# Finer first projections, an early half-sum of two score tiles and narrower last columns in a fused attention and gated MLP kernel

## The chip, the cores and the metric

The kernel runs on one NeuronCore of a Trainium2 chip. The metric is the device time of one execution in microseconds (us); the time before is the median of 3 runs, 195.9 us (195.79 to 197.63). The engines are named as in the profile: PE is the TensorE matrix engine, PEld its weight loads, DVE is VectorE, ACT is ScalarE, POOL is GpSimd and SP is SyncE, which here only issues DMAs.

## The reference

One transformer block on a sequence of S = 2048 rows, D = 512, in bf16:

```python
h  = x + attn(layernorm(x)) @ wo           # 32 heads of 16, q,k,v = layernorm(x) @ wqkv
h2 = h + (relu(h_n @ W_gate) * (h_n @ W_up)) @ W_down      # h_n = layernorm(h), F = 1376
# attn: row s looks at the 8 rows s, s-2, ..., s-14 (rows below 0 are masked)
logits = einsum("bhsd,bhswd->bhsw", q, k_gathered) * 16**-0.5
o      = einsum("bhsw,bhswd->bhsd", softmax(logits), v_gathered)
```

## The kernel before

**Chunks.** The rows are worked on in four chunks (0 to 3) of 512 rows. Activations lie transposed, features on the 128 partitions and rows along the free axis, in tiles of [128, 4, 512] called quad. A chunk passes through these steps; the names are those of the plan in the code, with the chunk's number behind a point (sc1.3 is step sc1 of chunk 3).

- xst, xag, xxn, xtp: layernorm of x and its transposition on PE (chunk 3's goes through SP's DMA transpose).
- qkv0 to qkv11 (line 572): the twelve projections of 128 output features, each 4 matmuls of 512 columns over the depth of 512. Numbers 0 to 7 are q and k in turn for feature group t = 0 to 3; 8 to 11 are v. ACT evicts each from its PSUM bank (line 580). In chunk 0 the first NHALF of the q, k projections are split in three parts, a (rows 0 to 255, depth parts 0 and 1), b (the same rows, depth parts 2 and 3) and c (rows 256 to 511), of 256 columns each, so that they can run before all rows are there.
- pr0, pr1 (line 620, in chunk 0 line 637 in halves): DVE multiplies q by four shifted copies of k into a tile big of [128, 8, 512]: two feature groups t, t+1 in one tile, four window places each. pr0 is for the window places 0 to 3, pr1 for 4 to 7. There are two such tiles for each.
- sc0, sc1 (line 628): PE sums the features of each head with a 0/1 matrix sel of 32 columns: 8 matmuls for a tile big, 16 for both, each on a quarter of the PE array's columns, into one bank. ex0, ex1 on ACT take exp of it.
- es (DVE, line 728) adds the two exp tiles and den (PE) sums them over the window with one matmul; a chunk that is not in DEN1 has no es, and den takes two matmuls instead (line 716). dl and dr (ACT) make the reciprocal; am0, am1 (DVE, line 740) multiply the exp tiles by it in chunks 1 to 3.
- bd0, bd1 (SP, line 756): 4 DMAs each copy the weights out to all features. mu0 to mu3 (DVE, line 788, in chunk 0 line 803): weights by v, four tiles big. ta (POOL, line 831) or tree (DVE, line 791) adds the upper half of a big to its lower half, and tree goes on to 1: chunks 0 to 2 do the first step by an accumulating DMA of POOL, chunk 3 on DVE.
- wo (line 867), rs, layernorm hnm, hsq, hxn (lines 448, 456, 502), transposition htp on PE or htd on SP, in parts.
- mm0 to mm5 (lines 940 and 907): gate and up, 4 matmuls of 512 columns each; mm5 is the tail of 96 features (line 907). ue and ge (ACT) evict, gu (DVE, line 968) multiplies. dn (line 990): down projection, four row blocks a chunk, each 11 matmuls, in a first part of 8 and a second of 3. o (DVE line 1003 or ACT line 999) adds the residual or evicts, os stores (line 1009 or 1027).

**The order.** Each step is an Op with an engine. RANK holds one number for each Op in the order of its creation; on each engine the Ops run in the order of their numbers, and nothing else moves one ahead of another. Buffers are given out by a plan with durations written in the code: 5 tiles big, 9 quad, 8 PSUM banks, 5 row, 3 ex. An engine that reaches a step whose input or buffer is not ready waits, and everything behind it on that engine waits too.

**The end.** In chunk 3 the last row block of dn is made in pieces of columns, cut at LASTC: 0 to 255 and 256 to 511, each with its own add (line 1003) and its own store.

PRH names pairs of q*k tiles, (chunk, pr0 or pr1, first feature group), whose two feature groups are added before sc: sc then takes 4 matmuls for the tile rather than 8. Before, PRH is empty. With "V" the add is done by DVE (line 654), in place.

Of the kernel before, what the change touches and what calls it, by code (L numbers as in the profile page):

```python
# [17 lines left out]
RANK = [  # L18
# [38 lines left out]
]  # L57


# [33 lines left out]
class Plan:  # L93
# [9 lines left out]
    def add(self, key, *a, **k):  # L103
        op = Op(*a, **k)
        op.key = key
        op.seq = len(self.ops)
        if RANK:
            op.prio = RANK[op.seq]
        self.ops.append(op)
        for b in set(op.take) | set(op.use):  # L110
            b.left += 1
        return op
# [90 lines left out]
def kernel(  # L203
# [12 lines left out]
    Bsz, S, D = A_x.shape  # L216
# [5 lines left out]
    W = 8  # L222
    DIL = 2
    PADL = 16
    DEN1 = (1, 2, 3)
    BCD = {(0,0):"SSSS",(0,1):"SSSS",(1,0):"SSSS",(1,1):"SSSS",(2,0):"SSSS",(2,1):"SSSS",(3,0):"SSSS",(3,1):"SSSS"}
    PRE = ()
    PRD = ()
    PRH = {}
    ODA = (0, 1)  # L230
    LATE = "ud"
    NAB = 0
# [64 lines left out]
    V = nc.vector  # L297
# [75 lines left out]
    PRS, MUH = (0,), (0,)  # L373
    TDD, TDL = 1.3, 1.5
    NWARM, NFILL = 56, (13, 10, 0)
    NHALF = 6
    XT = (3.47, 3.64, 5.45, 5.97, 8.4, 8.7, 9.25, 9.75, 15.9, 17.65)
    WT = (7.65, 7.65, 5.0, 13.7, 19.0, 24.95, 22.4, 28.8)
    DMAT = (('h',2,0),('h',2,2),('h',3,0),('h',3,2),('h',1,0),('x',3,0),('x',3,2))
# [12 lines left out]
    HSP = ()  # L392
    TMT = (0, 1, 2, 3)
    TTM, DTG, ATE = 0.0845, 0.35, 0.3
    LASTC = (D // 2,)

    LNA = ((0, 1, 0, 1), (0, 0, 0, 0))

# [156 lines left out]
    for tk in range(NCK):  # L555
# [10 lines left out]
        for n, (c, t) in enumerate(seq):  # L566
# [15 lines left out]
            wl = wload["qkv"[c]][0]  # L582
            if tk == 0 and n < NHALF:

# [21 lines left out]
        for hf in range(2):  # L606
            sc, ex = Buf(at_s), Buf(ex_s)
            scd, prd = [], []
            for t in range(0, NT, 2):
# [12 lines left out]

                hs = PRH.get((tk, hf, t))

# [62 lines left out]
            elif tk in MERGE:  # L687
                scd = [add(("sc%d" % hf, tk), "PE", (4 - sum((tk, hf, t) in PRH for t in (0, 2))) * MM + SW, lambda p=prd: [f() for _, _, f in p],
                           [a for a, _, _ in prd], apr, take=[sc], use=[b for _, b, _ in prd], lat=PEL)]
# [21 lines left out]
        def f_dn(exs=exs, dn=dn, tk=tk, es=None):  # L711
            if tk in DEN1:
                nc.tensor.matmul(dn.t[:], lhsT=(same if tk in EARLY else spread)[:], rhs=es.t[:], start=True, stop=True)  # L713
                return
            for hf in range(2):
                nc.tensor.matmul(dn.t[:], lhsT=(same if tk in EARLY else spread)[:], rhs=exs[hf].t[:], start=(hf == 0), stop=(hf == 1))  # L716
# [6 lines left out]

        if tk in DEN1:
            es = Buf(es_s)
# [250 lines left out]
        if tk == NCK - 1:  # L976
            cs = (0,) + LASTC + (D,)
            parts[-1:] = [(BPC - 1, a, b) for a, b in zip(cs, cs[1:])]
# [98 lines left out]
```

## Time and profile before

| | |
|---|---|
| median of 3 runs | 195.9 us |
| profiled execution, whole | 196.0 us |
| its span, first to last instruction | 193.7 us |
| granted TensorE clock | 1.000 |
| PE busy | 188.5 us (97%) |
| DVE busy | 147.2 us (76%) |
| ACT busy | 115.2 us (59%) |

A row of the timeline gives start, duration, engine, line, operation, shapes and how many instructions are merged in it; a row of the chain that ended last gives start, duration, engine and line. "[0.56 <-ACT kT L580]" means that the engine was idle for 0.56 us and that the last thing to release it was ACT's write of kT on line 580. A matmul's own duration (379 ns for 512 columns) is longer than the step from one matmul to the next, since matmuls overlap; the chain gives the steps.

### The profile page before, as it was taken

The page shows a single profiled execution, that of the slowest core. Times are in us where ns is not written, and L with a number is a line of the kernel's source. Part 1 is how long each engine was busy: PE and PEld are TensorE (multiplying, and loading weights), DVE is VectorE, ACT ScalarE, POOL GpSimd, SP SyncE. Part 2 cuts the span into 40 slices and gives each one's busy share as a digit, 9 for nine tenths or more (in the row PEclk, how much of TensorE's full clock was granted, in tenths as well). Part 3 has the DMA queues.
Part 4 walks back from the last instruction along what each step waited for, and adds up shares of the span by engine and source line. Part 5 has one row for each costly group of instructions (what it writes and reads, how often), then busy time and mean ns, then how long its engine had stood idle before and what let it go on. Part 6 is the DMA issues. An engine that isn't in the chain of part 4 may idle for free.

```text
span 193.7 us, 3083 instructions
## 1 busy us (share of the span) xinstructions
PE 188.5 (97%) x1120; PEld 99.0 (51%) x1139; DVE 147.2 (76%) x239; ACT 115.2 (59%) x241; POOL 17.4 (9%) x35
## 2 busy tenths in 40 slices
PE   7999999999999999999999999999999999999993
PEld 7986455555436435454444554444445444545452
DVE  6889999999999999999997679999564401134331
ACT  3489898965999673965156649623478712435500
POOL 3000002330000013100044001003000000000000
PEclk9999999999999999999999999999999999999999
DMA  6799564999902609917579974135101624001102
GB/s 205 242 296 376 138 155 93 192 196 260 353 5 49 171 14 199 191 33 170 122 143 194 180 192 90 29 80 94 18 0 27 162 58 135 0 27 54 30 23 86
DMA packets 25070, 24.61 MB, mean 127 GB/s; under 512 B 11136, under 2 KB 21344, under 8 KB 25056
## 3 DMA queue, kind: packets, MB, share of 16 engines
q1 hardware_dynamic: 22032, 16.23, 30.1%
q0 software_dynamic: 2304, 7.34, 20.8%
q10 hardware_dynamic: 720, 0.85, 1.2%
q8 instruction: 9, 0.15, 0.3%
q14 instruction: 5, 0.04, 0.1%
HBM read 8.42 MB, written 2.10 MB: 54 GB/s over the span
## 4 chain that ended last, share of the span: by engine, by line
PE 97%; ACT 1%; issue 1%; DVE 0%; ACTq 0%
PE bank L940 35%; PE bank L572 21%; PE bank L990 20%; PE bank L867 7%; PE bank L628 4%; PE bank L421 3%; PE bank L907 3%; PE bank L531 2%; PE bank L429 1%; ACT up_sb L944 1%; PE bank L870 0%; PE bank L713 0%; PE bank L716 0%; DVE row L1003 0%; ACT vT L580 0%
## 5 line engine op out<-in xcount | busy, mean ns | idle before, releaser
L940 PE MATMUL bank<-quad,wgu_sb 128*128 128x512 bf16 x312 | 72.4, 379 | 0.4
L940 PEld LDWEIGHTS <-wgu_sb 128*128 128x128 bf16 x320 | 31.0, 98 | 36.4 <-issue 1.0
L990 PE MATMUL bank<-wd_sb,gT 128*128 128x512 bf16 (+2 forms) x185 | 39.6, 366 | 0.1
L944 ACT CAST up_sb<-bank 128x512 bf16<-128x512 f32 x40 | 22.3, 590 | 22.2 <-PE bank L940 20.5
L572 PE MATMUL bank<-quad,wqk_sb 128*128 128x512 bf16 (+1 forms) x148 | 29.4, 344 | 0.3
L947 ACT ACTIVATE gr<-bank 128x512 bf16<-128x512 f32 x40 | 23.5, 606 | 9.5 <-PE bank L940 5.2
L968 DVE TENSOR_TENSOR gT<-gr,up_sb 128x1024 bf16<-128x1024 bf16 x20 | 13.8, 688 | 19.4 <-ACT up_sb L944 10.5
L990 PEld LDWEIGHTS <-gT 128*128 128x128 bf16 (+1 forms) x187 | 18.2, 98 | 19.8 <-DVE gT L968 0.2
L620 DVE TENSOR_TENSOR big<-quad,kT 128x4096 bf16<-128x4096 bf16 x12 | 27.2, 2284 | 0.2 <-ACT kT L580 0.2
L788 DVE TENSOR_TENSOR big<-big,vT 128x4096 bf16<-128x4096 bf16 x12 | 27.1, 2285 | 0.2 <-PE bank L940 0.2
L572 PEld LDWEIGHTS <-wqk_sb 128*128 128x128 bf16 x152 | 16.7, 113 | 10.3 <-issue 0.2
L831 POOL DMA_DIRECT2D big<-big x12 | 10.5, 904 | 81.7 <-DVE big L788 54.2
L791 DVE TENSOR_TENSOR big<-big 128x1024 bf16<-128x1024 bf16 (+2 forms) x24 | 16.9, 728 | 0.0
L572 PE MATMUL bank<-quad,wv_sb 128*128 128x512 bf16 x61 | 15.3, 380 | 0.2
L867 PE MATMUL bank<-wo_sb,quad 128*128 128x512 bf16 x62 | 15.0, 379 | 0.1
L1003 DVE TENSOR_TENSOR row<-x_sm,bank 128x512 bf16<-128x512 bf16 (+1 forms) x9 | 5.5, 627 | 12.2 <-PE bank L990 12.2
L456 ACT ACTIVATE row<-x_sm,mv 128x512 bf16<-128x512 bf16 x12 | 8.6, 718 | 7.2 <-DVE mv L448 7.1
L547 ACT COPY quad<-bank 128x1024 bf16<-128x1024 bf16 (+1 forms) x10 | 8.6, 898 | 7.2 <-PE bank L531 7.2
L878 DVE SCALAR_TENSOR_TENSOR x_sm<-x_sm,bank 128x512 bf16<-128x512 bf16 x12 | 8.2, 687 | 4.9 <-PE bank L867 4.7
L580 ACT CAST kT<-bank 128x512 bf16<-128x512 f32 x16 | 9.1, 597 | 3.3 <-PE bank L572 1.8
L467 DVE BATCH_NORM_STATS2 st<-x_sm 128x6 f32<-128x512 bf16 x16 | 10.2, 675 | 0.4 <-DMA x_sm<-in_A_x_dram 0.4
L580 ACT CAST quad<-bank 128x512 bf16<-128x512 f32 x16 | 9.5, 602 | 1.6 <-PE bank L572 1.5
(77 smaller groups left out, 169.5 us busy)
## 6 DMA issues: line engine op xcount, KB each, us to landing
big<-big POOLq DMA_DIRECT2D x12, 512.0 KB, 5.3
big<-ex SPq DMA_DIRECT2D x32, 128.0 KB, 2.8
wgu_sb<-in_B_W_gate_dram SPq DMA_DIRECT2D x2, 688.0 KB, 7.7
wgu_sb<-in_B_W_up_dram SPq DMA_DIRECT2D x2, 688.0 KB, 7.5
wd_sb<-in_B_W_down_dram SPq DMA_DIRECT2D x2, 640.0 KB, 7.9
x_sm<-in_A_x_dram SPq DMA_DIRECT2D x2, 512.0 KB, 5.1
x_sm<-up_sb POOLq DMA_DIRECT2D x4, 256.0 KB, 3.8
out_dram<-x_sm SPq DMA_DIRECT2D x4, 256.0 KB, 2.3
```

Of the source, the lines that this page charges most:

```text
L572: nc.tensor.matmul(mm.t[:, lo:hi], lhsT=wv_sb[:, dt, t:D:NT] if c == 2 else wqk_sb[:, dt, c * D + t:(c + 1) * D:NT], rhs=xnT.t[:, dt, lo:h ...
L580: nc.scalar.copy(out=o, in_=mm.t[:])
L620: V.tensor_tensor(out=pb.t[:].rearrange("p (t w) s -> p t w s", t=2), in0=q4, in1=k4, op=ALU.mult)
L788: V.tensor_tensor(out=mt.t[:], in0=ab.t[:], in1=v8, op=ALU.mult)
L791: V.tensor_tensor(out=mt.t[:, 0:n, :], in0=mt.t[:, 0:n, :], in1=mt.t[:, n:2 * n, :], op=ALU.add)
L831: nc.gpsimd.dma_start(mt.t[:, 0:4, :], mt.t[:, 4:8, :], accum_op=ALU.add)
L867: nc.tensor.matmul(od.t[:], lhsT=OT.t[:, t, j * P:(j + 1) * P], rhs=wo_sb[:, t, :], start=(t == 0), stop=(t == NT - 1 and tk not in RPE))
L940: nc.tensor.matmul(mm.t[:fs, lo:hi], lhsT=wgu_sb[:, dt, g, ft * P: ft * P + fs], rhs=hnT.t[:, dt, lo:hi], start=(dt == 0), stop=(dt == NT ...
L944: nc.scalar.copy(out=ub.t[:fs, i, :], in_=um.t[:fs, :])
L947: nc.scalar.activation(out=gr.t[:fs, i, :], in_=gm.t[:fs, :], func=ACT.Relu)
L968: V.tensor_tensor(out=gt.t[:fs, 0:n, :], in0=gr.t[:fs, 0:n, :], in1=ub.t[:fs, 0:n, :], op=ALU.mult)
L990: nc.tensor.matmul(od.t[:, c0:c1], lhsT=gts[ft].t[:fs, ft % 2, j * P:(j + 1) * P], rhs=wd_sb[:fs, ft, c0:c1], start=(ft == 0), stop=(ft == ...
```

## The change

Four settings and the order change; no function's text does.

```diff
 RANK = [
     0, 1, 2, 3, 4, 5, 6, 7, 8, 9, 10, 11, 12, 13, 14, 15, 16, 17, 18, 19,
     20, 22, 23, 25, 29, 31, 32, 21, 24, 26, 28, 30, 36, 39, 40, 27, 33, 35, 37, 42,
-    47, 51, 34, 38, 41, 43, 46, 50, 55, 44, 56, 69, 77, 64, 65, 76, 79, 48, 53, 60,
...
+    47, 51, 34, 38, 41, 43, 46, 50, 54, 77, 81, 87, 92, 79, 84, 85, 89, 53, 57, 59,
...
-    DEN1 = (1, 2, 3)
+    DEN1 = (0, 1, 2, 3)
...
-    PRH = {}
+    PRH = {(3, 1, 0): 'V', (3, 1, 2): 'V'}
...
-    NHALF = 6
+    NHALF = 8
...
-    LASTC = (D // 2,)
+    LASTC = (D // 2, 3 * D // 4)
```

All eight q, k projections of chunk 0 are now in three parts, where q and k of feature group 3 (numbers 6 and 7) were whole. Chunk 0 gets an es like the other chunks. Chunk 3's two pr1 tiles are each added half to half by DVE before sc1.3. The last row block ends in pieces of 256, 128 and 128 columns. RANK is a new list with 11 more entries, so most steps change their place. Three places of it follow.

DVE, the q*k products of chunk 0 (line 637, a half tile each; the tiles big are numbered), with the statistics of other rows around them (lines 467 and 470, 488 for chunk 1). Before:

```order
L637 TENSOR_TENSOR big_88<-quad_80,kT 128x2048
L488 SCALAR_TENSOR_TENSOR nb_126<-mv_119,rs_131 128x4
L637 TENSOR_TENSOR big_89<-quad_80,kT 128x2048 x2
L637 TENSOR_TENSOR big_90<-quad_80,kT 128x2048 x2
L637 TENSOR_TENSOR big_88<-quad_80,kT 128x2048
L637 TENSOR_TENSOR big_91<-quad_80,kT 128x2048
L699 TENSOR_TENSOR ex_100<-ex_100,mask 128x16
L637 TENSOR_TENSOR big_91<-quad_80,kT 128x2048
```

Now:

```order
L637 TENSOR_TENSOR big_88<-quad_80,kT 128x2048
L488 SCALAR_TENSOR_TENSOR nb_126<-mv_119,rs_131 128x4
L637 TENSOR_TENSOR big_89<-quad_80,kT 128x2048
L637 TENSOR_TENSOR big_90<-quad_80,kT 128x2048
L637 TENSOR_TENSOR big_91<-quad_80,kT 128x2048
L637 TENSOR_TENSOR big_88<-quad_80,kT 128x2048
L637 TENSOR_TENSOR big_90<-quad_80,kT 128x2048
L637 TENSOR_TENSOR big_91<-quad_80,kT 128x2048
L637 TENSOR_TENSOR big_89<-quad_80,kT 128x2048
L699 TENSOR_TENSOR ex_100<-ex_100,mask 128x16
```

Products for both groups of window places now alternate feature group by feature group (1 and 3 first, which are projections 2, 3, 6, 7), and all eight stand ahead of the mask of the first exp tile.

DVE between chunk 1's layernorm (line 502) and chunk 3's pr1 products (line 620) with the new adds (line 654); line 788 is chunk 2's weights by v, 791 and 825 its trees. Before:

```order
L620 TENSOR_TENSOR big_88<-quad_85,kT 128x4096
L502 TENSOR_SCALAR row_106<-x_sm,mv_119,rs_131 128x512
L502 TENSOR_SCALAR row_105<-x_sm,mv_119,rs_131 128x512
L502 TENSOR_SCALAR row_109<-x_sm,mv_119,rs_131 128x512
L502 TENSOR_SCALAR row_108<-x_sm,mv_119,rs_131 128x512
L788 TENSOR_TENSOR big_92<-big_89,vT 128x4096
L788 TENSOR_TENSOR big_91<-big_89,vT 128x4096
L788 TENSOR_TENSOR big_88<-big_89,vT 128x4096
```

Now:

```order
L788 TENSOR_TENSOR big_90<-big_88,vT 128x4096
L502 TENSOR_SCALAR row_109<-x_sm,mv_119,rs_131 128x512
L502 TENSOR_SCALAR row_106<-x_sm,mv_119,rs_131 128x512
L502 TENSOR_SCALAR row_107<-x_sm,mv_119,rs_131 128x512
L502 TENSOR_SCALAR row_108<-x_sm,mv_119,rs_131 128x512
L788 TENSOR_TENSOR big_92<-big_88,vT 128x4096
L788 TENSOR_TENSOR big_89<-big_88,vT 128x4096
L788 TENSOR_TENSOR big_91<-big_88,vT 128x4096
L620 TENSOR_TENSOR big_88<-quad_87,kT 128x4096
L791 TENSOR_TENSOR big_92<-big_92 128x1024
L825 TENSOR_TENSOR quad_82<-big_92 128x512
L620 TENSOR_TENSOR big_92<-quad_87,kT 128x4096
```

Both pr1.3 products have gone from ahead of chunk 2's four mu to behind them. What follows on DVE now are a gu and the two adds:

```order
L968 TENSOR_TENSOR gT_99<-gr_112,up_sb_111 128x1024
L654 TENSOR_TENSOR big_88<-big_88 128x2048
L654 TENSOR_TENSOR big_92<-big_92 128x2048
L791 TENSOR_TENSOR big_89<-big_89 128x1024
L791 TENSOR_TENSOR big_90<-big_90 128x1024
```

On PE sc1.3 moves with them: it stood between chunk 1's wo and chunk 1's first gate and up steps, and now stands behind 13 of those steps, with 8 matmuls rather than 16.

70 rows, old and new, of the table RANK are left out of this document.

## The prediction

> **What bounds the kernel now.** I first read the busy times by stretch, since a share over the whole span would mix stages. The columns are the stretch, its length, then the busy time of PE, PEld, DVE, ACT and POOL, the granted clock and the DMA share.
>
> ```profile
> core 0: us, PE busy (x) PEld busy (x) DVE busy (x) ACT busy (x) POOL busy (x), PEclk, DMA share, GB/s
> 8.40:60.00 51.60, 51.24 (x342) 28.71 (x348) 50.38 (x76) 42.52 (x87) 4.76 (x7) 1.00 0.74 199
> 60.00:100.00 40.00, 39.64 (x242) 19.02 (x246) 39.58 (x51) 24.34 (x50) 5.11 (x6) 1.00 0.60 124
> 100.00:140.00 40.00, 39.79 (x193) 18.81 (x195) 33.75 (x53) 21.99 (x47) 5.28 (x7) 1.00 0.59 114
> 140.00:181.00 41.00, 40.79 (x208) 20.01 (x210) 13.91 (x33) 21.38 (x47) 0.00 (x0) 1.00 0.20 55
> ```
>
> From 8.4 us on PE is idle for 0.36, 0.36, 0.21 and 0.21 us, 1.14 us in all. So the time is PE's work plus a head and a tail, and the change can win only by giving PE less work, by the tail, and at most by those 1.14 us. DVE is as full as PE until 100 us, with 1.22 and 0.42 us to spare, and has 6.25 us to spare from 100 to 140. It cannot win time, but where it is late PE waits.
>
> Second, the chain that ended last. It runs on PE almost throughout, which gives the true step from matmul to matmul, and it shows the tail.
>
> ```profile
> 9.72 3.50 PE bank L572 x32
> ...
> 17.99 0.98 PE bank L628 x16
> ...
> 29.48 0.43 PE bank L716 x2
> ...
> 36.46 10.96 PE bank L572 x50
> ...
> 61.05 0.89 PE bank L531 x16
> ...
> 86.42 1.51 PE bank L867 x7
> ...
> 89.88 5.18 PE bank L990 x24
> ...
> 110.64 0.66 PE bank L907 x8
> ...
> 181.11 9.56 PE bank L990 x55
> 190.66 0.02 issue
> 190.69 0.42 DVE row L1003
> ```
>
> A matmul of 512 columns takes 5.18/24 = 0.216 us, of 256 columns 3.50/32 = 0.109, of 128 columns (the transposes, each with weights of its own) 0.89/16 = 0.056. Below, a group of four 512s is 0.863 us.
>
> **The change, part by part.** The sum is made against the profiled execution, 196.0 us with a span of 193.7; the median shown is 195.9, 0.1 lower.
>
> *Half-sum of chunk 3's pr1 tiles.* PE loses 8 of the 16 matmuls of a 0.98 us row: -0.49. DVE gains two adds of 128x2048 (below): +2.44, which cost nothing while sc1.3 is not reached before them.
>
> *es for chunk 0.* PE does one matmul of 0.43/2: -0.21. DVE gains one add of 0.42, in the stretch where it has 1.22 us to spare.
>
> *Projections 6 and 7 in parts.* Each was 4 x 0.216 = 0.86 and is now 8 x 0.109 = 0.87: nothing.
>
> *Last pieces of 128.* 11 matmuls of 256 columns, 1.20, become 22 of 128, 22 x 0.056 = 1.22: +0.02. Behind the last matmul stand an add and a store.
>
> ```profile
> L1003 DVE TENSOR_TENSOR row<-x_sm,bank 128x512 bf16<-128x512 bf16 x7 | 4.6, 686 | 10.9 <-PE bank L990 10.9
> ...
> L1003 DVE TENSOR_TENSOR row<-x_sm,bank 128x256 bf16<-128x256 bf16 x2 | 0.8, 422 | 1.3 <-PE bank L990 1.3
> ...
> L728 DVE TENSOR_TENSOR row<-ex,ex 128x512 bf16<-128x512 bf16 x3 | 1.3, 419 | 0.0
> ...
> L791 DVE TENSOR_TENSOR big<-big 128x2048 bf16<-128x2048 bf16 x4 | 4.8, 1218 | 0.0
> ```
>
> ```profile
> big<-ex SPq DMA_DIRECT2D x32, 128.0 KB, 2.8
> ...
> out_dram<-row SPq DMA_DIRECT2D x7, 128.0 KB, 1.7
> ...
> quad<-row SPq DMA_TRANSPOSE x14, 2.4
> ...
> out_dram<-row SPq DMA_DIRECT2D x1, 64.0 KB, 1.5
> ```
>
> 256 fewer columns took 0.264 off the add, so 128 fewer should take 0.13: 0.29 (at worst 0.42, at best 0.21). No row shows a store of 32 KB with 256 bytes a row. The step from 128 to 64 KB was worth 0.2 us; the next may be worth 0.1, and a store of small pieces may be slower, at the dearest two such stores in turn, 1.5 us more. I take 0, near the 64 KB row.
>
> Of the Trainium skill, one rule speaks against these pieces: "TensorE: Matmul & The Clock Gate", section "Back-to-back issue gap", gives some 81 ns a matmul for a stream of loads and matmuls of N=128, and 131 for N=512. By it the 22 would take an estimated 1.78 us, 0.56 more. The trace disagrees with both figures here: 56 ns for 128 and 216 for 512.
>
> Sum: -0.49 - 0.21 + 0.02 - 0.13 = **-0.81 us**, if PE meets no new wait.
>
> **Does the new order make PE wait?** Almost every step has moved, so I laid the new lists of PE and DVE side by side at the places where PE takes what DVE has just made, with the steps of the trace. First chunk 0's scores.
>
> ```profile
> 12.18 1.23 DVE L637 TENSOR_TENSOR big<-quad,kT 128x2048 bf16<-128x2048 bf16 x1 [0.56 <-ACT kT L580]
> ...
> 13.39 6.89 DVE L637 TENSOR_TENSOR big<-quad,kT 128x2048 bf16<-128x2048 bf16 x6
> ```
>
> Ahead of the first product PE does as many parts as before (four a, three b, then c of projections 2 and 3), so DVE starts at 12.18 again. sc1.0 needs the sixth product: 12.18 + 0.15 (line 488) + 6 x 1.15 = 19.2. PE reached sc1.0 at 17.99; now one more v projection and three more sets of four transposes stand ahead (0.86 + 0.67): 19.5. Margin 0.3 us. The es of chunk 0 delays DVE by 0.42 and is needed at den.0, nine projections and two score steps later.
>
> Next sc1.3, counted from wo.1, which began at 86.42.
>
> ```profile
> 86.26 3.62 PE L867 MATMUL bank<-wo_sb,quad 128*128 128x512 bf16 x15
> 86.46 5.19 SPq L756 DMA_DIRECT2D big<-ex  x8
> ...
> 90.53 0.15 DVE L448 TENSOR_SCALAR mv<-sm 128x1 f32<-128x1 f32 x1
> ...
> 93.12 1.38 DVE L502 TENSOR_SCALAR row<-x_sm,mv,rs 128x512 bf16<-128x512 bf16 x4
> 93.88 2.52 SPq L520 DMA_TRANSPOSE quad<-row  x2
> 94.41 6.69 DVE L788 TENSOR_TENSOR big<-big,vT 128x4096 bf16<-128x4096 bf16 x3
> ```
>
> PE: 16 matmuls of wo and 36 of dn.0 (52 x 0.216 = 11.2), 8 transposes (0.45), 13 gate and up groups (11.2), two tails (1.3): sc1.3 at 110.6. DVE, from 90.6 where wo.1's residuals end: four mu and two products of 2.23, four row scalings (1.38), one tree (1.0), one gu (0.69), two adds (2.44): 109.5. Margin 1.1 us. Inside this, chunk 1's first gate and up step now starts at 98.2 (before, sc1.3 stood ahead of it). It needs two DMA transposes, issued from 93.88: the second starts at 95.1 and lands 2.4 later, 97.5. Margin 0.7.
>
> Then wo.3, which needs chunk 3's whole attention. This part moves late: am0 and am1 of chunk 3 ended at 107.15, and now come 5.7 us behind sc1.3 (den, two ACT steps, es, gu), at 116.3. The rows of before around them:
>
> ```profile
> 103.93 0.86 POOL L831 DMA_DIRECT2D big<-big  x1 [1.68 <-DVE big L788]
> ...
> 106.24 8.66 SPq L756 DMA_DIRECT2D big<-ex  x8
> ...
> 106.73 0.42 DVE L740 TENSOR_TENSOR ex<-ex,rec 128x512 bf16<-128x512 bf16 x1
> ...
> 117.85 2.28 DVE L788 TENSOR_TENSOR big<-big,vT 128x4096 bf16<-128x4096 bf16 x1
> ...
> 136.84 0.75 DVE L825 TENSOR_TENSOR quad<-big 128x512 bf16<-128x512 bf16 x2
> ...
> 138.57 2.75 PE L867 MATMUL bank<-wo_sb,quad 128*128 128x512 bf16 x12
> ```
>
> The eight copying DMAs need 5.2 us to issue if they go as chunk 2's did (5.19), the last lands 2.8 later: mu can start at 123.7. Four mu (8.9), the trees (4.9 + 2.6 + 1.4) and a gu (0.6): 142.1. PE behind sc1.3 has half a score step, seven gate and up groups, den, wo.2, dn.1, 13 more groups and two tails, 32.3 us: wo.3 at 142.9. Margin 0.8 us; before it was 1.0, from 137.6 to 138.6. Behind wo.3, seven gate and up groups and all of dn.2, 15.5 us, cover its layernorm.
>
> All margins are positive, but four of them lie between 0.3 and 1.1 us, and each is the difference of sums of some 20 us. I allow 0.3 us for small waits: 196.0 - 0.81 + 0.3 = 195.5, and 0.1 less against the median: **195.4 us**.
>
> **Rivals.**
> *The gain is eaten at the handovers.* The earlier PE is, the sooner it stands before DVE, which is full until 100 us and gets 0.42 us more there. If DVE sets the pace up to sc1.3, the 0.21 of den and the spare 0.3 and 0.7 are lost: waits of 0.8 us or a little more, 195.8 to 196.4. For it speaks DVE's 39.58 of 40 us; against it, that the margins come out positive.
>
> *Chunk 3's broadcasts are slow again: slower.* Before, the eight DMAs took 8.66 us to issue instead of 5.19, in a stretch where POOL's accumulating DMAs ran too. If they do so at their new place, mu starts 3.5 us later, and past the margin of 0.8 PE waits 2.7 at wo.3: 198.1. It decides as soon as the issue takes over 6 us. Against it: the last of POOL's accumulations for chunk 2 was issued at 103.93, 2 us before the broadcasts; now it follows its mu at about 101, 15 us before them.
>
> *The weight loads bound the last pieces.* A load of 128x128 behind line 990 takes 98 ns by its row. If matmuls of 128 columns wait for theirs, 22 take 2.16 us, 0.94 more than counted: 196.3.
>
> ```profile
> L990 PEld LDWEIGHTS <-gT 128*128 128x128 bf16 x170 | 16.6, 98 | 17.9 <-DVE gT L968 0.2
> ```
>
> The transposes, with loads as long, ran at 56 ns, so it is unlikely. The section of the Trainium skill named above would give 0.56 of these 0.94.
>
> *The old pauses go.* If the new order also loses the 1.14 us of idle time: 196.0 - 0.81 - 1.14 - 0.1 = 193.9, the best possible.
>
> **How the numbers follow.** Forecast (195.0 to 195.8) 0.50; eaten 0.26; slow broadcasts 0.13; weight loads 0.05; pauses gone 0.06. The range leaves out the slow broadcasts and the best case and takes in the dearer store: **194.8 to 197.2**. One per cent, 1.96 us, is about what a measurement can tell from no change. Faster by more needs the whole of the best case: 0.02. Slower by more needs the slow broadcasts: 0.10 of their 0.13. Within: 0.88.
>
> **What the profile after would show.** PE's busy time down by 0.7 us; idle time by stretch near 0.3 us each; sc1.3 as 8 matmuls in half a microsecond near 110, DVE's line 654 twice at 1.2 us; the last add 0.29 and matmuls of 128 columns 0.056 apart. It would be wrong if a stretch shows PE idle for over a microsecond, most likely ahead of wo.3 with the eight DMAs of line 756 spread out, or ahead of a first gate and up step behind DMA transposes.

## The result

The changed kernel takes 198.1 us (median of 20 runs, 196.73 to 200.61), the kernel before 196.3 us beside it (20 runs, 195.63 to 197.63): a ratio of **1.0073, with an interval of 1.0052 to 1.0095**. It is slower by 0.7%, where 195.4 us was forecast. That is inside the one per cent either way to which most of the chance was given, but the time lies above the range of 194.8 to 197.2 us. The ratio leaves out three slow runs of the changed kernel (199.82 us and more), so it is not simply that of the two medians.

The profiled execution of the changed kernel took 197.48 us with a span of 195.5 us, at a granted clock of 1.00. Its busy times by stretch, with the columns as before (PE, PEld, DVE, ACT, POOL):

```profile
8.40:60.00 51.60, 49.40 (x331) 28.98 (x336) 48.64 (x75) 40.15 (x83) 8.99 (x7) 1.00 0.74 198
60.00:100.00 40.00, 39.55 (x241) 18.74 (x244) 37.96 (x51) 25.69 (x55) 3.98 (x5) 1.00 0.56 116
100.00:140.00 40.00, 39.79 (x198) 18.54 (x200) 36.69 (x49) 22.05 (x47) 6.44 (x8) 1.00 0.63 122
140.00:181.00 41.00, 40.79 (x208) 19.99 (x210) 17.90 (x40) 21.21 (x46) 0.00 (x0) 1.00 0.21 58
```

PE is idle for 2.20, 0.45, 0.21 and 0.21 us; before it was 0.36, 0.36, 0.21 and 0.21. So the loss lies ahead of 60 us. DVE is not fuller there but emptier: 48.64 us of work in the stretch, where it had 50.38. And POOL is busy for 8.99 us in place of 4.76.

The chain that ended last no longer runs on PE alone. Between chunk 0's den (line 713 at 30.42) and chunk 1's (59.72) it leaves PE for POOL, DVE and ACT, and from 66.85 to 88.61 once more for DMAs and DVE, where PE itself waited only 0.24 us in the end (for DVE's line 825, ahead of wo.1):

```profile
8.50 0.60 PE bank L572 x4
...
30.42 0.22 PE bank L713
...
43.03 5.08 POOL wgu_sb L849
...
53.30 0.94 ACT x_sm L876 x3
...
59.72 0.38 PE bank L713
...
62.80 1.15 PE bank L531 x16
...
88.61 3.63 PE bank L867 x16
...
113.02 0.55 PE bank L628 x8
...
183.04 9.59 PE bank L990 x66
...
192.65 0.29 DVE row L1003
```

I added up PE's list of matmuls at the steps that the rows of the prediction give (0.216 us for 512 columns, 0.109 for 256, 0.056 for 128, 0.061 for a matmul of sc, 0.083 for one of the tail of 96 features). From the first projection to the last matmul that is 181.46 us before and 180.80 after, 0.66 less. PE took 190.67 - 8.46 = 182.21 and 192.63 - 8.50 = 184.13. So it stood still for 0.75 us before and **3.33 us** after: 2.58 us of new waits against 0.66 of saved work. The steps are rounded, so each of these sums is good to some 0.4 us; the difference between the two kernels does not hang on that. Counted by the same sums to places on the way, the waits after were nothing up to den.0 and up to wo.0 (48.73, a row below), 2.03 at den.1, 2.20 at chunk 0's transposes (62.80), 2.90 at wo.1 (88.61) and 3.09 at sc1.3 (113.02); before they were 0.29 at the transposes and 0.56 at wo.1. Between wo.0 and den.1, within 11 us, PE lost 2 us; the trace shows 0.44 and 1.27 of it as waits.

The timeline of the changed kernel at that place:

```profile
42.89 2.28 DVE L620 TENSOR_TENSOR big<-quad,kT 128x4096 bf16<-128x4096 bf16 x1
43.03 5.08 POOL L849 COPY wgu_sb<-big 1x4 bf16<-1x4 bf16 x1 [3.08 <-DVE big L791]
...
48.30 4.49 DVE L620 TENSOR_TENSOR big<-quad,kT 128x4096 bf16<-128x4096 bf16 x2 [0.24 <-POOL wd_sb L850]
...
48.73 1.03 PE L867 MATMUL bank<-wo_sb,quad 128*128 128x512 bf16 x4
...
52.82 0.58 ACT L580 CAST kT<-bank 128x512 bf16<-128x512 f32 x1 [2.33 <-DVE big L620]
...
53.30 0.60 ACT L876 ACTIVATE x_sm<-bank 128x512 bf16<-128x512 f32 x1
...
54.03 0.15 DVE L448 TENSOR_SCALAR mv<-sm 128x1 f32<-128x1 f32 x1 [1.24 <-ACT x_sm L876]
...
54.60 0.15 DVE L448 TENSOR_SCALAR mv<-sm 128x1 f32<-128x1 f32 x1 [0.42 <-ACT x_sm L876]
...
57.42 1.02 PE L572 MATMUL bank<-quad,wv_sb 128*128 128x512 bf16 x4 [0.44 <-ACT ex L696]
...
59.25 0.42 DVE L728 TENSOR_TENSOR row<-ex,ex 128x512 bf16<-128x512 bf16 x1
...
59.72 0.38 PE L713 MATMUL bank<-row,same 128*128 128x512 bf16 x1 [1.27 <-DVE row L728]
```

Read it backwards. PE waits 1.27 us at den.1 for es.1 (line 728). DVE was late with es.1 because it had stood still for 1.24 and 0.42 us at two instructions of one element per partition, the means of chunk 0's second layernorm (hnm.0, line 448). These waited for ACT's residual sums (rs.0, line 876), though their banks had been ready: wo.0 had begun at 48.73. ACT was standing at 52.82, behind a wait of 2.33 us, to evict the k projection of chunk 2's feature group 2 (line 580). And that waited for DVE's products of chunk 1 (line 620). The exps of chunk 1 (line 696) stand behind it in ACT's queue too: PE waited 0.44 us for the first of them at 57.42, and the second ended only at 58.53, so es.1 could not have begun before that even on a DVE that was on time.

The eviction's wait is one that the data don't need. The product reads kT at the columns of chunk 1 and the 14 before; the eviction writes columns of chunk 2. But one product takes two feature groups, and the range of its reads, from the first element to the last, spans the rest of the first group's columns. The 2.33 us in the trace fit this reading; experiments 4 and 7 test it. Before, the same kind of wait stood in ACT's queue, 1.48 us long, but with nothing behind it that DVE or PE needed soon:

```profile
41.08 0.60 POOL L849 COPY wgu_sb<-big 1x4 bf16<-1x4 bf16 x1 [1.60 <-DVE big L791]
...
44.99 0.59 ACT L580 CAST kT<-bank 128x512 bf16<-128x512 f32 x1 [1.48 <-DVE big L620]
```

The first of these rows, from the kernel before, shows the other difference: POOL's copy of four elements took 0.60 us there and 5.08 after, and its end is what DVE's next product waits for, by 0.24 us.

### The profile page after: what moved, and what is told of

The parts are those of the page before. It is cut to its first block, busy times and chain, and to the rows that moved or that the text cites. A ratio compares the mean times of both kernels' runs of the same rounds, so it can differ in the third digit from the quotient of the medians.

```text
span 195.5 us, 3098 instructions
## 1 busy us (share of the span) xinstructions
PE 188.5 (96%) x1131; PEld 99.9 (51%) x1149; DVE 151.3 (77%) x243; ACT 115.0 (59%) x241; POOL 21.6 (11%) x35
## 4 chain that ended last, share of the span: by engine, by line
PE 77%; DVE 11%; DMA 5%; POOL 3%; issue 2%; ACT 1%; DVEq 0%; ACTq 0%
PE bank L940 27%; PE bank L990 19%; PE bank L572 16%; PE bank L867 5%; DVE big L620 5%; DVE big L788 4%; DMA big<-big 3%; PE bank L421 3%; POOL wgu_sb L849 3%; PE bank L531 2%; PE bank L907 2%; PE bank L628 2%; DMA big<-ex 2%; PE bank L429 1%; ACT x_sm L876 1%
## 5 line engine op out<-in xcount | busy, mean ns | idle before, releaser
L940 PE MATMUL bank<-quad,wgu_sb 128*128 128x512 bf16 x312 | 71.6, 379 | 0.4
L990 PE MATMUL bank<-wd_sb,gT 128*128 128x512 bf16 (+3 forms) x195 | 39.3, 355 | 0.2
L572 PE MATMUL bank<-quad,wqk_sb 128*128 128x512 bf16 (+1 forms) x157 | 30.0, 336 | 0.4 <-issue 0.2
L620 DVE TENSOR_TENSOR big<-quad,kT 128x4096 bf16<-128x4096 bf16 x12 | 27.2, 2285 | 0.3 <-POOL wd_sb L850 0.2
L572 PEld LDWEIGHTS <-wqk_sb 128*128 128x128 bf16 x160 | 17.4, 113 | 10.2 <-issue 1.3
L1003 DVE TENSOR_TENSOR row<-x_sm,bank 128x512 bf16<-128x512 bf16 (+2 forms) x10 | 5.4, 578 | 10.4 <-PE bank L990 10.3
L580 ACT CAST kT<-bank 128x512 bf16<-128x512 f32 x16 | 9.3, 598 | 5.4 <-PE bank L572 3.1
L572 PEld LDWEIGHTS <-wv_sb 128*128 128x128 bf16 x64 | 7.1, 114 | 8.2 <-issue 2.7
L580 ACT CAST vT<-bank 128x512 bf16<-128x512 f32 x16 | 9.2, 620 | 2.8 <-remote 1.9
```

What stands on the lines that cost most here:

```text
L572: nc.tensor.matmul(mm.t[:, lo:hi], lhsT=wv_sb[:, dt, t:D:NT] if c == 2 else wqk_sb[:, dt, c * D + t:(c + 1) * D:NT], rhs=xnT.t[:, dt, lo:h ...
L580: nc.scalar.copy(out=o, in_=mm.t[:])
L620: V.tensor_tensor(out=pb.t[:].rearrange("p (t w) s -> p t w s", t=2), in0=q4, in1=k4, op=ALU.mult)
L940: nc.tensor.matmul(mm.t[:fs, lo:hi], lhsT=wgu_sb[:, dt, g, ft * P: ft * P + fs], rhs=hnT.t[:, dt, lo:hi], start=(dt == 0), stop=(dt == NT ...
L990: nc.tensor.matmul(od.t[:, c0:c1], lhsT=gts[ft].t[:fs, ft % 2, j * P:(j + 1) * P], rhs=wd_sb[:fs, ft, c0:c1], start=(ft == 0), stop=(ft == ...
```

## The experiments

Two theories stood against each other. A: the wait in ACT's queue starves hnm.0, es.1 and den.1. B: POOL's long copy holds DVE up, and the rest follows from that. A third question was whether the settings or the order are to blame. All kernels compute the whole reference; each was timed in 5 rounds beside the kernel before, and ratios are to that.

**1. The residual sums ahead of the eviction.** In the changed kernel, only RANK is touched: ACT's k eviction steps back behind three of the four residual sums. ACT's queue:

```diff
 L580 CAST vT<-bank 128x512
-L580 CAST kT<-bank 128x512
 L876 ACTIVATE x_sm,sm<-bank 128x512
 L876 ACTIVATE x_sm,sm<-bank 128x512
 L580 CAST quad<-bank 128x512
+L876 ACTIVATE x_sm,sm<-bank 128x512
+L580 CAST kT<-bank 128x512
 L456 ACTIVATE row,sq<-bank,mv 128x512
-L876 ACTIVATE x_sm,sm<-bank 128x512
```

> The changed kernel with two steps of ACT's order moved: the eviction of chunk 2's third k group (line 580) goes behind three of chunk 0's residual sums (line 876) instead of ahead of them. Theory A (ACT's queue: that eviction waits 2.33 us for DVE's products, and the sums behind it hold DVE for 1.24 + 0.42 us and PE for 0.44 + 1.27): DVE no longer waits for line 876, PE's wait for line 728 falls below 0.4 us, and the time falls by about 1.5 us against the changed kernel, to within 0.3 us of the kernel before. Theory B (POOL's copy of line 849, 5.08 us, holds a tile big and the weight loads): no change, ratio to before still 1.007. Theory C (DVE is simply too full): the wait at line 728 stays.

Measured: ratio **0.9989 (0.9950 to 1.0028)**. The timeline at the same place:

```profile
43.03 5.08 POOL L849 COPY wgu_sb<-big 1x4 bf16<-1x4 bf16 x1 [3.08 <-DVE big L791]
...
48.29 4.49 DVE L620 TENSOR_TENSOR big<-quad,kT 128x4096 bf16<-128x4096 bf16 x2 [0.24 <-POOL wd_sb L850]
...
52.70 0.21 DVE L448 TENSOR_SCALAR mv<-sm 128x1 f32<-128x1 f32 x2
...
53.47 2.29 DVE L620 TENSOR_TENSOR big<-quad,kT 128x4096 bf16<-128x4096 bf16 x1 [0.56 <-ACT kT L580]
...
58.47 0.38 PE L713 MATMUL bank<-row,same 128*128 128x512 bf16 x1 [0.60 <-DVE row L728]
```

POOL's copy is as long as ever and DVE's product waits for it as before. But hnm.0 runs without a wait, 1.3 us earlier, and den.1 starts at 58.47. The loss is gone with a move in ACT's queue alone. That is A. What is left at den.1, 0.60, comes from the moved eviction, which the next product now waits for.

**2. POOL's copies read another tile.** Their only use is to hold two weight loads back until a step is done, so they can read any tile of the right moment:

```diff
-in_=mt.t[0:1, 0:1, 0:NT]
+in_=OT.t[0:1, NT - 1:NT, 0:NT]
```

> The changed kernel, with POOL's two small copies (lines 849, 850) reading the attention output tile (quad) instead of a tile big, so that DVE's product at 48.30 no longer waits for POOL; the copies may still be slow. Theory A: DVE starts 0.25 us earlier there, which ends at the same wait on ACT: 0.2 us faster at most. Theory B: 1.5 us faster or more.

Measured: **1.0025 (0.9988 to 1.0062)**. The copy got longer, and DVE did not wait for it any more:

```profile
45.08 6.94 POOL L849 COPY wgu_sb<-quad 1x4 bf16<-1x4 bf16 x1 [5.62 <-DVE quad L795]
...
47.48 4.49 DVE L620 TENSOR_TENSOR big<-quad,kT 128x4096 bf16<-128x4096 bf16 x2
...
51.99 0.58 ACT L580 CAST kT<-bank 128x512 bf16<-128x512 f32 x1 [1.84 <-DVE big L620]
53.20 0.15 DVE L448 TENSOR_SCALAR mv<-sm 128x1 f32<-128x1 f32 x1 [1.24 <-ACT x_sm L876]
...
58.89 0.38 PE L713 MATMUL bank<-row,same 128*128 128x512 bf16 x1 [1.27 <-DVE row L728]
```

DVE's wait for POOL is gone, and the waits of ACT, of hnm.0 and of den.1 (1.27) all stand. So B is not the cause. The copy's 0.24 us is a term of its own; the interval of this ratio reaches down to that of a kernel without loss and up into that of the change, so it doesn't size the term more closely.

**3. Both together.** The edits of 1 and 2.

> Both edits: ACT's order as in x1_rs_first and POOL's copies as in x2_lg_ot. Theory A: 1.7 us faster than the changed kernel, at or just below the kernel before (ratio 0.998 to 1.001), PE idle from 8.4 to 60 us back to about 0.5 us. Theory B: as x2_lg_ot alone. If neither: the ratio stays at 1.007.

Measured: 0.9970 (0.9940 to 1.0000), not to be told from 1.

**4. Chunk 1's products one feature group at a time.** This takes away what makes the eviction wait: a product of one group reads a range in which no column of chunk 2 lies.

```diff
-PRS, MUH = (0,), (0,)
+PRS, MUH = (0, 1), (0,)
```

Chunk 1 then has eight products of line 637 where it had four of line 620, each pair in the old one's place; the order is otherwise that of the change.

> The changed kernel with chunk 1's q*k products made in halves, one feature group each, as chunk 0's are (line 637 instead of 620), nothing else moved. A product then reads one group's columns, and the eviction of the next chunk's k carries no wait for DVE. DVE has four more instructions, about 0.3 us. Theory A: ACT's 2.33 us wait is gone, DVE's 1.66 us behind it too, and the time falls by about 1.2 us against the changed kernel. If the eviction waited for something real that is late anyway (theory C), the time rises by up to 0.3 us.

Measured: **0.9967 (0.9941 to 0.9993)**. In its trace the eviction waits for DVE no more:

```profile
44.47 5.14 POOL L849 COPY wgu_sb<-big 1x4 bf16<-1x4 bf16 x1 [3.15 <-DVE big L791]
...
51.72 0.62 ACT L580 CAST kT<-bank 128x512 bf16<-128x512 f32 x1
...
54.35 0.21 DVE L448 TENSOR_SCALAR mv<-sm 128x1 f32<-128x1 f32 x2
...
59.47 0.38 PE L713 MATMUL bank<-row,same 128*128 128x512 bf16 x1 [0.36 <-DVE row L728]
```

The eviction and hnm.0 wait for nothing, again with POOL's copy as long. Two different edits, one that only moves the wait out of the way and one that removes it, each bring the time back to that of the kernel before: the cause is settled as A. That the wait comes from the range of the product's reads rests on this experiment and on experiment 7.

**5. Two settings alone, in the old order.** The kernel before, with es for chunk 0 and the pieces of 128.

```diff
-DEN1 = (1, 2, 3)
+DEN1 = (0, 1, 2, 3)
-LASTC = (D // 2,)
+LASTC = (D // 2, 3 * D // 4)
```

> The kernel before, with two of the settings and its own order: es for chunk 0 (one DVE add ahead of the first mu, one matmul of den less) and the last row block in pieces of 256, 128 and 128 columns, narrow ones last. By the forecast's terms: PE loses 0.21 us and gains 0.02, the last add takes 0.29 instead of 0.42 us: 0.2 to 0.35 us faster (ratio 0.998 to 0.999). If the settings themselves cost (weight loads behind the narrow matmuls, 0.94 us more; DVE too full for one add): 0.4 to 1 us slower. The 22 matmuls of 128 columns should step by 0.056 us.

Measured: 0.9990 (0.9962 to 1.0017). No wait of PE appears behind the head, and the end is that of the change (a row of the windows, then two of the chain):

```profile
8.40:60.00 51.60, 51.23 (x348) 28.77 (x352) 50.80 (x77) 42.87 (x89) 4.76 (x7) 1.00 0.74 200
...
181.49 9.59 PE bank L990 x66
191.10 0.29 DVE row L1003
```

From the first projection (8.90) to the end of its span (193.8) it took 184.9 us, where before took 193.7 - 8.46 = 185.2: 0.3 less, as 0.21 and 0.13 less 0.03 say. The runs cannot tell that from nothing.

**6. The half-sum alone, in the old order.** The kernel before, with the two adds of line 654 directly behind chunk 3's second pr1 product.

```diff
-PRH = {}
+PRH = {(3, 1, 0): 'V', (3, 1, 2): 'V'}
```

> The kernel before, with chunk 3's pr1 tiles added half to half by DVE directly behind the second product, where DVE has no room; nothing else moves. PE loses 0.49 us, DVE gains 2.44 us ahead of chunk 1's row scalings. If DVE paces PE there: PE waits ahead of sc1.3 or of chunk 1's transpositions for most of 2.44 us, and the time rises by 1 to 2 us. If DVE's time is free: 0.5 us faster.

Measured: **1.0107 (1.0063 to 1.0151)**. Its windows and timeline:

```profile
60.00:100.00 40.00, 38.38 (x228) 18.30 (x232) 39.24 (x52) 23.78 (x48) 3.60 (x5) 1.00 0.56 116
...
93.70 2.36 DVE L654 TENSOR_TENSOR big<-big 128x2048 bf16<-128x2048 bf16 x2
...
96.12 0.40 PE L628 MATMUL bank<-big,sel 128*32 128x512 bf16 x4 [0.26 <-DVE big L654]
...
97.41 0.62 PE L531 MATMUL bank<-identity,row 128*128 128x128 bf16 x8 [0.90 <-DVE row L502]
```

PE is idle for 1.62 us in the stretch where DVE had 0.42 to spare. The half-sum cannot be had in the old order: it saves PE 0.49 us and costs more where DVE is full. So a new order was needed for this one part.

**7. The new order with the four old settings.**

```diff
-DEN1 = (0, 1, 2, 3)
+DEN1 = (1, 2, 3)
-LASTC = (D // 2, 3 * D // 4)
+LASTC = (D // 2,)
-PRH = {(3, 1, 0): 'V', (3, 1, 2): 'V'}
+PRH = {}
-NHALF = 8
+NHALF = 6
```

> The changed kernel's order with all four settings as before (no half-sums, no es for chunk 0, six projections in parts, two last pieces). Theory A (the order alone costs, by ACT's queue at 50 us): PE's wait for line 728 and DVE's wait for line 876 are there as in the changed kernel, and the time is that of the changed kernel plus about 0.6 us of PE work, less up to 0.4 for the es: ratio to before 1.008 to 1.011. If the settings cost: at or below 1.002.

Measured: **1.0080 (1.0044 to 1.0116)**, the loss of the change without any of its parts. The order costs it. Not by quite the same waits, though: hnm.0 does not wait in its profile, and instead DVE's fourth product of chunk 1 waits for the k eviction, which itself waited for nothing:

```profile
49.09 2.29 DVE L620 TENSOR_TENSOR big<-quad,kT 128x4096 bf16<-128x4096 bf16 x1 [0.25 <-POOL wd_sb L850]
...
51.97 0.62 ACT L580 CAST kT<-bank 128x512 bf16<-128x512 f32 x1
...
52.62 2.29 DVE L620 TENSOR_TENSOR big<-quad,kT 128x4096 bf16<-128x4096 bf16 x1 [1.24 <-ACT kT L580]
...
59.95 0.38 PE L713 MATMUL bank<-row,same 128*128 128x512 bf16 x1 [0.58 <-DVE row L728]
```

It is the same pair of steps turned round. In the plan of the change the eviction of group 2 comes directly behind the product of groups 2 and 3, and waits for it; with the old settings the plan puts it directly ahead, and the product waits. The data need neither wait, and each cost DVE 1.24 us or more.

Its profiled execution was also one in which x came late (the last section), so its waits cannot all be put down to the order.

**8. The copies on ACT.** Experiment 1, with the two tiny copies done by ACT at the same moment.

```diff
-nc.gpsimd.tensor_copy(out=wgu_sb[0:1, :, 1, 0:1], ...
+nc.scalar.copy(out=wgu_sb[0:1, :, 1, 0:1], ...
```

> As x1_rs_first, with the two small copies of lines 849 and 850 done by ACT instead of POOL. If POOL's copy of four elements took 5.08 us because DVE's back-to-back instructions kept it off the SBUF port, ACT's takes 0.2 to 0.4 us, the weight loads behind it start at about 43.5 instead of 48.1 us, and DVE's 0.24 us wait for line 850 is gone: 0.2 to 0.3 us faster than x1_rs_first. If the copy waits for something else (the accumulating DMA), it is as late on ACT, and holds ACT's queue: 1 us slower or more.

Measured: 1.0004 (0.9967 to 1.0040), no gain over experiment 1. The copies took 0.21 and 0.23 us on ACT, and DVE's product waited for no one. POOL's 5 us were nearly free.

**9. The change again, and two more mends.** The change itself, unaltered, was run once more beside the halves of experiment 4 with the copies on ACT, and beside the halves with the move of experiment 1.

> The changed kernel itself, unaltered, beside the kernels that mend it, on one chip. Theory (a false wait in ACT's queue at 50 to 53 us starves den.1): 1.007 of before again, PE idle about 2.2 us before 60 us, with the 1.27 us at den.1 among them. Rival (chips or executions differ, and the earlier loss was of that call): within 0.3% of before.

> The change with chunk 1's products made one group at a time (which removes the false wait) and with the two tiny copies of lines 849 and 850 on ACT in place of POOL. Theory: the copies are off every chain once the eviction waits no more, so this equals the halves alone, 0.9967 of before (0.994 to 0.999), with PE idle before 60 us near 0.9 us or less. Rival (POOL's long copy still costs something, through the weight loads of up projection that SP issues behind it, 5 us late): 0.994, with the loads issued at 43 in place of 48 us and PE idle less after 60 us.

> The change with both cures: chunk 1's products made one group at a time, and the residual sums of line 876 ahead of chunk 2's third k eviction in ACT's queue. Theory: one cause, two cures, so both together give what either gives: 0.997 of before (0.994 to 1.000), PE idle before 60 us 0.9 to 1.3. Rival (each removes a part of the loss of its own): 0.995 or less, and no PE wait behind line 728.

Measured: the change 1.0086 (1.0049 to 1.0122), with the wait of 1.3 us at den.1 again; the halves with copies on ACT **0.9973 (0.9940 to 1.0006)**; the halves with the move 1.0015 (0.9984 to 1.0045), no better than either cure alone, where 0.997 was expected. The halves with copies on ACT show PE's work without the loss (a row of the windows and one of the chain):

```profile
8.40:60.00 51.60, 51.09 (x343) 29.74 (x345) 50.71 (x80) 42.68 (x91) 3.78 (x5) 1.00 0.73 198
...
58.06 0.28 PE bank L713
```

PE is idle for 0.51 us up to 60, and den.1 waits for nothing.

All profiled executions side by side. "Waits" is PE's time from the first projection to the last matmul, less its work by the steps; "span behind" is the span less the start of the first projection; "DVE behind" is the start of DVE's first q*k product behind the first projection.

| kernel | ratio | waits, us | span behind, us | DVE behind, us |
|---|---|---|---|---|
| before | 1 | 0.75 | 185.2 | 3.7 |
| the change | 1.0073 | 3.33 | 187.0 | 3.7 |
| the change again | 1.0086 | 2.60 | 186.3 | 3.7 |
| 1 sums ahead | 0.9989 | 1.58 | 185.2 | 3.7 |
| 2 other tile | 1.0025 | 2.34 | 185.9 | 3.8 |
| 3 both | 0.9970 | 3.12 | 186.8 | 4.8 |
| 4 halves | 0.9967 | 2.96 | 186.7 | 4.9 |
| 5 two settings | 0.9990 | 0.91 | 184.9 | 3.7 |
| 6 half-sum | 1.0107 | 3.42 | 187.7 | 3.7 |
| 7 order | 1.0080 | 3.99 | 188.5 | 5.8 |
| 8 copies on ACT | 1.0004 | 1.47 | 185.1 | 3.7 |
| 9 halves, ACT | 0.9973 | 1.07 | 184.7 | 3.7 |
| 9 halves, sums ahead | 1.0015 | 3.61 | 187.2 | 5.8 |

In the rows with 3.7 or 3.8 the ratio goes with the waits: up to 1.6 us it is 0.997 to 1.000, at 2.34 it is 1.0025, and from 2.6 on 1.007 to 1.011. In the four rows with 4.8 or more a late load of x hides it; there only the ratio, from many runs, speaks.

The best are the halves: they (4) and the halves with copies on ACT beat the change by 1.1%, and stand 0.3% ahead of the kernel before. Only for 4 does the interval stop short of 1, by less than 0.1%, so a gain over the kernel before is hardly shown.

## Why the prediction was wrong

**The bound** was read rightly: PE nearly without a gap, DVE as full until 100 us, and so "where it is late PE waits". That is what happened.

**The terms of the sum** came out. sc1.3 takes 0.55 us for 8 matmuls where it took 0.98 (-0.43; -0.49 forecast). den.0 is one matmul of 0.22 (-0.21), and by PE's sums nothing was lost up to it, the projections in parts included. The last pieces: 9.59 us for 66 matmuls where 55 took 9.56, so +0.03 for +0.02. Of the Trainium skill's figure for matmuls of 128 columns ("TensorE: Matmul & The Clock Gate", section "Back-to-back issue gap"), by which they would have cost an estimated 0.56 us more, nothing shows. The last add took 0.29 us as said. The two stores of 32 KB left the tail as it was, 195.5 - 192.65 - 0.29 = 2.6 us, where 193.7 - 190.69 - 0.42 made 2.6.

**The step that failed** is "Does the new order make PE wait?". It laid only PE's and DVE's lists side by side, at the places where PE takes what DVE has made in chunk 0's scores, in sc1.3, in chunk 1's gate and up and in wo.3, and added 0.3 us for small waits. The new waits came to 2.58. Each handover that was checked held. sc1.0 started at 19.59 with no wait (19.5 by the sum). sc1.3 started at 113.02 in place of 110.6, 2.2 of the 2.4 us being lost by wo.1 (88.61 in place of 86.42); DVE's second half-sum had ended at 112.1, so its margin was 0.9 (1.1 forecast). The last tile for wo.3 (line 825) ended at 144.9 and PE came at 145.44: 0.5 (0.8). Three rows of the timeline and one of the chain:

```profile
109.79 2.35 DVE L654 TENSOR_TENSOR big<-big 128x2048 bf16<-128x2048 bf16 x2
...
118.45 5.13 SPq L756 DMA_DIRECT2D big<-ex  x8
...
144.15 0.75 DVE L825 TENSOR_TENSOR quad<-big 128x512 bf16<-128x512 bf16 x2
...
145.44 3.45 PE bank L867 x16
```

The one that failed was not on the list: chunk 1's scores, with es.1 for den.1, through a loop of three engines. What set the loop off is a wait between two steps that share no data, a k eviction and a product. DVE's list alone would have shown no lateness: its two waits there, 1.24 and 0.42 us, were for ACT. ACT's queue was not looked at; it was 82% busy in this stretch before (42.52 of 51.60 us). But a queue with slack still holds up everything behind one waiting instruction, and the prediction's own row for chunk 0 ("0.56 <-ACT kT L580") and the row at 44.99 above had shown that k evictions wait and are waited for. The order of ACT's queue should have been checked for each step that DVE takes from it.

**The rivals.** "The gain is eaten at the handovers" had the right sign and the right engines, PE before DVE ahead of 100 us, but took DVE's fullness for the cause and 0.8 us for the size. DVE was idle when it happened. "Chunk 3's broadcasts are slow again" gives 198.1 us, the very number measured, and yet did not happen: the eight DMAs of line 756 were issued in 5.13 us (5.19 assumed for the forecast, 8.66 for the rival). "The old pauses go" and "the weight loads" did not come either.

**With the wait mended the sum fits.** The halves with copies on ACT are the change plus the removal of the two things it hit. Behind the first projection its profiled span is 184.7 us, where before has 185.2: 0.5 us less, which is what -0.81 + 0.3 promised; the ratio of 0.9973 is 0.5 us too, though its interval reaches just past 1. The forecast gain was lost in one loop of waits, which began between two instructions.

## What to carry to other kernels

When an order changes, walk every engine's queue, not only that of the bound and its feeder: for each instruction that the full engines wait for, see what stands ahead of it on its engine and what that waits for in turn. A wait that costs nothing today is marked in the trace all the same ("1.48 <-DVE big L620" with no harm behind it); note each such wait on a half-idle engine, and check what the new order puts behind it. If an instruction waits for a reader that shares no element with what it writes, look at the span of addresses that the reader covers, and cut the reader into pieces before arranging the order around it.

## What the runs showed of the hardware that was not expected

**A copy of four elements took 5 to 7 us on POOL.** It took 0.60 us before, 5.08 in the change and 6.94 in experiment 2, and ended each time when DVE, which was running two-input operations back to back, paused (48.05 and 51.95). On ACT it took 0.21. The Trainium skill, "SBUF — State Buffer", section "Who interferes with whom", says that a DVE instruction with two SBUF inputs contends with a GpSimd instruction that reads SBUF, and that the port pair the two engines share is an exclusive lock. The traces agree that the copy is held, and show more: it was held across several DVE instructions in a row, each of 2.3 us at most, and not until the first of them ended. It is not only a matter of the profile's spans on POOL: SP issued the weight loads that wait for the copies from 48.14 in the change and from 43.09 in experiment 8. That the ports are the reason is argued; no run here separates them from other causes on POOL. It cost the time little: with the copies on ACT (experiment 8) there was no measurable gain.

**The load of x varies between executions.** DVE's first q*k product starts 3.7 us behind the first projection in nine of the thirteen profiled executions and 4.8 to 5.8 us behind in the other four, where DVE's statistics waited for x. In experiment 4:

```profile
11.20 1.88 DVE L467 BATCH_NORM_STATS2 st<-x_sm 128x6 f32<-128x512 bf16 x3 [1.15 <-DMA x_sm<-in_A_x_dram]
```

All four kernels with a late load have the new order, but so do six without, and the runs don't show whether the order has a part in it. It is why one profiled time cannot rank these kernels: experiments 3 and 4 have the best ratios and long profiled spans.
